# Causal masks from 64 rows in the attention scores of a fused attention and expert kernel

## The chip, the cores and the metric

The kernel runs on one core of a Trainium2 chip. A core has a matrix engine (PE, with its weight loads shown apart as PEld), a vector engine (DVE), a scalar engine (ACT), a general engine (POOL), and a queue engine (SP) that starts the transfers here. Each engine works through its own instructions in order, and engines wait for each other by semaphores. The metric is the time of one execution on the device in microseconds (us); the number compared is a median over runs.

## The reference

What must be computed, cut to what matters:

```python
# 4 batches, 12 heads, 448 positions, 64 dimensions for each head
scores = scale * np.matmul(q, k.transpose(0, 1, 3, 2))
mask = np.triu(np.ones((seq, seq), dtype=bool), k=1)
scores = np.where(mask, -1000000000.0, scores)
scores = scores - np.max(scores, axis=-1, keepdims=True)
attn = np.exp(scores)
attn = attn / (np.sum(attn, axis=-1, keepdims=True) + 1e-09)
x = np.matmul(attn, v)            # then (1792 tokens, 768)
h = np.maximum(np.maximum(x @ w1, x @ w2), x @ w3)
out = h @ w_out
```

Row m of the scores may only see columns up to m. All inputs are float32.

## The kernel before

The 48 heads are worked in 24 pairs; the two heads of a pair lie side by side on the partitions, head 0 on rows 0 to 63 and head 1 on rows 64 to 127. The 448 positions make four blocks of rows: 0, 1 and 2 with 128, and 3 with 64. For each pair the scores come in two groups, each into a PSUM tile S of two banks, one bank for each head:

- Group A (z = 0, function `mm` in `attend`, line 710): blocks 2 (384 columns at 0) and 0 (128 columns at 384).
- Group B (z = 1): block 1 (256 columns at 0) of each head, and block 3 of both heads at once: the 64 last rows of head 0 and of head 1 stand as 128 output rows, with 256 keys in one bank and 192 in the other.

The causal mask is a matrix product that goes into the same PSUM area ahead of the scores: a bf16 identity `identb` (128 × 128) as weights times a constant mask `mk` that holds 0 or −2^104 as the moving operand; the scores then accumulate on top. In group A this is one product of 256 columns for each head (two copies of the 128 × 128 mask, for the diagonals of blocks 2 and 0). In group B it is one of 128 columns for each head, and one for block 3. The scores themselves are fp32; those of blocks 0, 1 and 2 have 64 rows of weights, one head on the upper half of PE's rows and the other on the lower half; those of block 3 have 128 rows.

```python
for h in range(2):
    m(512 * h + 256, 256, identb, mk[:, 0:256], True)      # group A, line 719
...
m(896, 128, identb, mk[:, 256:384])                        # group B, line 723
```

Behind the scores DVE takes the maxima (line 741), ACT the exponentials with their sums (line 752); the first 6 pairs are then transposed on PE (line 766), the later ones are split into two 16-bit halves and transposed by a DMA (line 808). The products with the values fill a tile O (line 828, 16-bit, or 841 for the first pairs): weights of 128 rows and 64 columns, the two heads on different columns of PE. Between them PE works through the hidden products of the experts (line 1030) and the output products (line 1441), and after the last pair through two schemes of combined products for the other batches (lines 1262 and 1387); all these have weights of 128 rows and 128 columns.

What runs when is written down: `ORDER` is a list of all operations and `ENGINE` says which engine takes each. A planner (class `Order`) goes through that list with a cost for each operation and works out a start time, the buffer that each result gets, and the order by start time in which the program is emitted. The cost of the two groups of scores stands ahead of line 733.

The masks are prepared at the start (lines 1507 to 1519) by POOL, while PE runs 13 products of no use on the tile `junk` (line 1501).

Of the kernel before, what the change touches and what calls it, by code (L numbers as in the profile page):

```python
# [9 lines left out]
BF16 = mybir.dt.bfloat16  # L10
I32 = mybir.dt.int32
AF = mybir.ActivationFunctionType
ALU = mybir.AluOpType
AX = mybir.AxisListType

P = 128
D = 64
# [157 lines left out]
    qr=3, kr=3, acc=2, p32=2, ph=2, pT=3, v16=5, vr=4, w3=4, x=4, wst=2, h=6, hacc=4, osb=2, S=2, O=1, M=3,  # L175
# [16 lines left out]
class Order:  # L192
# [31 lines left out]
    def add(self, cost, emit, reads=(), writes=(), ring=None, prio=0.0, lat=None, chain=None, bank=None, port=False):  # L224
        i = len(self.ops)
        deps, behind = set(), set()
        for n in reads:
            deps.update(self.writers.get(n, ()))
        for n in writes:
            deps.update(self.writers.get(n, ()))  # L230
            deps.update(self.readers.get(n, ()))
        for z in (chain, ring[0] if ring and ring[0] in self.FIFO else None):
            if z is not None:
                if z in self.last:
                    behind.add(self.last[z])
                self.last[z] = i
        for n in reads:
            self.readers.setdefault(n, []).append(i)
        for n in writes:
            self.writers[n] = [i]  # L240
            self.readers[n] = []
        if ring is not None:
            self.ring_of[ring[1]] = ring[0]
            if len(ring) == 2:
                self.pending[ring[0]] = self.pending.get(ring[0], 0) + 1
        names = set()
        for n in list(reads) + list(writes) + ([ring[1]] if ring else []):
            names.add(n)
            if isinstance(n, tuple) and isinstance(n[0], tuple):
                names.add(n[0])  # L250
        names = {n for n in names if n in self.ring_of}
        for n in names:
            self.uses[n] = self.uses.get(n, 0) + 1
        self.ops.append(dict(cost=cost, emit=emit, deps=deps, behind=behind - deps, ring=ring, prio=prio, lat=lat, names=names, bank=bank, port=port, group=self.group))
# [146 lines left out]
def c_pe(*cols):  # L401
    return sum(n / 2400 + 0.003 for n in cols)


def c_pe32(*cols):
    return sum(4 * n / 2400 + 0.006 for n in cols)


def c_dma(*parts):

    issue = [0.45 for _ in parts]
    data = sum(n * z for n, z in parts) / 340e3
    return [(e, 0.06 * len(parts), sum(issue), data, False, sum(issue[:-1])) for e in ("sp", "act")]
# [7 lines left out]
def attention_moe(ctx: ExitStack, tc: tile.TileContext, q, k, v, w1, w2, w3, wo, out):  # L421
    nc = tc.nc
    PE, ACT, DVE, POOL, SP = nc.tensor, nc.scalar, nc.vector, nc.gpsimd, nc.sync
# [3 lines left out]
    c1 = ctx.enter_context(tc.tile_pool(name="c1", bufs=1))  # L427
    psp = ctx.enter_context(tc.tile_pool(name="psp", bufs=1, space=PSUM))
    shapes = dict(
        qr=([P, 512], F32), kr=([P, S_LEN], F32), acc=([P, 28], F32), p32=([P, 1024], F32), ph=([P, 16, P], F16),  # L430
# [57 lines left out]
    identb = c1.tile([P, P], BF16, name="identb")  # L488


    mk = c1.tile([P, 3 * P], BF16, name="mk")
    junk = c1.tile([P, 384], F16, name="junk")
    osc = c1.tile([P, 8], F32, name="osc")
    tiny = osc[:, 4:6]
# [14 lines left out]
    add = od.add  # L509
# [4 lines left out]
    def ap(t, off, dims, p0=0, np_=P):  # L514
        s = t.ap[0][0]
        return bass.AP(t.tensor, t.offset + p0 * s + off, [[s, np_]] + [list(d) for d in dims])
# [179 lines left out]
    def attend(b, p, prio, plain):  # L696
        qr, kr, acc, O = ((n, b, p) for n in ("qr", "kr", "acc", "O"))
# [3 lines left out]
        for z, blocks in enumerate(HALVES):  # L701
            od.group = f"{'ab'[z]}{6 * b + p}"
            S, y = ("S", b, p, z), ("p32", b, p, z)
            pr = prio + 0.1 * z
# [5 lines left out]
            def mm(e, z=z, S=S):  # L710
                o, qq, kk = T(S), T(qr), T(kr)

                def m(c, w, l, r, start=False):
                    PE.matmul(o[:, c : c + w], l, r, start=start, stop=True, skip_group_check=True)  # L714


                if z == 0:
                    for h in range(2):
                        m(512 * h + 256, 256, identb, mk[:, 0:256], True)
                else:  # L720
                    for h in range(2):
                        m(512 * h + 128, 128, identb, mk[:, 0:P], True)
                    m(896, 128, identb, mk[:, 256:384])
                    m(256, 256, qq[:, 384:512], kk[:, 0:256])
                    m(768, 192, qq[:, 384:512], kk[:, 256:448])
                for i, c in ((2, 0), (0, 384)) if z == 0 else ((1, 0),):
                    w = P * (i + 1)
                    for h in range(2):
                        hs = slice(D * h, D * h + D)
                        m(512 * h + c, w, qq[hs, P * i : P * i + P], kk[hs, 0:w])  # L730

            cost = c_pe(256, 256) + c_pe32(384, 128) if z == 0 else c_pe(128, 128, 128) + c_pe32(256, 192, 256)
            add([("pe", cost + (0.3 if z == 0 else 0.36))], mm, reads=[qr, kr], writes=[S], ring=("S", S), prio=pr)

            groups = [blocks[0:2], blocks[2:4]] if z == 0 else [blocks[0:2], blocks[2:3]]
            for gi, g in enumerate(groups):

                def mx(e, g=g, S=S):
# [6 lines left out]
                    ring=("acc", acc) if z == 0 and gi == 0 else None, prio=pr, chain=acc, bank=S)  # L745
# [3 lines left out]
            for n, at, parts, c, w in blocks:  # L749

                def ex(e, at=at, parts=parts, c=c, w=w, S=S, y=y):
# [6 lines left out]
                    writes=[(y, n, "e"), (acc, "s", n)], ring=("p32", y) if first else None, prio=pr, chain=y, bank=S)  # L758

            if plain:  # L760
                for g in range(2):
# [6 lines left out]
                    def place(e, g=g, M=M, t=t):  # L768
# [4 lines left out]
                    c = dict(act=c_act(512, -0.09), dve=c_dve(512))  # L773
                    add([(e, c[e]) for e in ENGINES["pT"]], place, reads=[M], writes=[(t, 0, g), (t, 1, g)],
                        ring=("pT", t) if g == 0 else None, prio=pr + 0.4, bank=M, chain=t)
                continue

            def eps(e, cols=cols):
# [4 lines left out]
                writes=[(acc, "r", z)], prio=pr)  # L783
# [12 lines left out]
            def p_lo(e, z=z, y=y):  # L796
# [4 lines left out]
                prio=pr, port=True)  # L801
# [5 lines left out]
            def tr(e, z=z):  # L807
# [3 lines left out]
                ring=("pT", pT[z]), prio=prio + 0.4)  # L811
# [38 lines left out]
        if plain:  # L850
# [18 lines left out]
            def quotient(e):  # L869
# [4 lines left out]
            c = dict(act=c_act(S_LEN, 0.02), dve=c_dve(S_LEN) + 0.06)  # L874
            add([(e, c[e]) for e in ENGINES["R"]], lambda e: scaled(e, T(x32), T(R)[:, 0:S_LEN], bsc[:, b, 10:11]),
                reads=[R, ("scale", b)], writes=[x32], ring=("hacc", x32), prio=prio + 0.6)
            add([("pe", 4 * c_pe(*(6 * [P] + 4 * [D])) + 0.1)], pv_plain, reads=pb + vb, writes=[O], ring=("O", O),
                prio=prio + 0.9)
            add([("dve", c_dve(S_LEN))], quotient, reads=[O], writes=[x32], prio=prio + 0.9)
            add([("act", c_act(S_LEN, -0.045))], lambda e: scaled(e, T(x)[:, kx, 0], T(x32), 1.0), reads=[x32],  # L880
                writes=[(x, kx, 0)], ring=("x", x) if kx == 0 else None, prio=prio + 0.9, chain=x)
            add(c_rest("x lo", S_LEN), lambda e: rest(e, T(x)[:, kx, 1], T(x32), T(x)[:, kx, 0]), reads=[x32, (x, kx, 0)],
                writes=[(x, kx)], prio=prio + 0.9, port=True)
            return

        for z in range(2):
            add([("pe", 3 * c_pe(*(4 * [P] if z == 0 else 2 * [P] + 4 * [D])) + (0.02 if z == 0 else 0.12))], lambda e, z=z: pv(e, z),
                reads=[n for n in pb if n[0] == pT[z]] + vb + [(O, 0)] * z, writes=[(O, z)], ring=("O", O) if z == 0 else None,
                prio=prio + 0.9)
# [614 lines left out]
    DVE.memset(bsc, 0.0)  # L1504
    DVE.memset(tiny[:, 0:1], 1e-9 / PS)
    DVE.memset(tiny[:, 1:2], 1e-9)
    POOL.memset(mk, 0.0)
    for t in (ident, identb):
        POOL.memset(t, 1.0)
    for z in range(2):  # L1510
        POOL.affine_select(
            out=mk[:, P * z : P * z + P], in_=mk[:, P * z : P * z + P], pattern=[[-1, P]], base=0, channel_multiplier=1,
            compare_op=ALU.is_ge, fill=-(2.0**104))
    for t in (identb, ident):
        POOL.affine_select(
            out=t, in_=t, pattern=[[-1, P]], base=0, channel_multiplier=1, compare_op=ALU.is_equal, fill=0.0)
    for h in range(2):
        POOL.tensor_copy(mk[D * h : D * h + D, 256 : 256 + D], mk[0:D, 0:D])
    POOL.memset(mk[:, 256 + D : 384], -(2.0**104))


    u = 0
# [56 lines left out]
```

## Time and profile before

| | |
|---|---|
| median of 3 runs | 464.23 us (463.53 to 465.03) |
| the profiled execution's own time | 464.76 us |
| its span, first to last instruction | 463.1 us |
| mean granted clock of PE | 0.995 |
| PE busy | 453.9 us (98%) |
| DVE busy | 415.0 us (90%) |
| ACT busy | 323.2 us (70%) |
| POOL busy | 149.2 us (32%) |

The span is what the profile covers; the execution's own time has 1.7 us around it. Busy times of PE count each product from its start to the end of its way through the array, so products that follow each other overlap, and the distance from one start to the next tells more than one duration. An fp32 product appears as two instructions. In the chain of waits the profile goes back from the last instruction, at each step to what released it.

### The profile page before, as it was taken

The page shows a single profiled execution, that of the slowest core. Times are in us where ns is not written, and L with a number is a line of the kernel's source. Part 1 is how long each engine was busy: PE and PEld are TensorE (multiplying, and loading weights), DVE is VectorE, ACT ScalarE, POOL GpSimd, SP SyncE. Part 2 cuts the span into 40 slices and gives each one's busy share as a digit, 9 for nine tenths or more (in the row PEclk, how much of TensorE's full clock was granted, in tenths as well). Part 3 has the DMA queues.
Part 4 walks back from the last instruction along what each step waited for, and adds up shares of the span by engine and source line. Part 5 has one row for each costly group of instructions (what it writes and reads, how often), then busy time and mean ns, then how long its engine had stood idle before and what let it go on. Part 6 is the DMA issues. An engine that isn't in the chain of part 4 may idle for free.

```text
span 463.1 us, 9807 instructions
## 1 busy us (share of the span) xinstructions
PE 453.9 (98%) x3705; PEld 266.1 (57%) x3705; DVE 415.0 (90%) x801; ACT 323.2 (70%) x760; POOL 149.2 (32%) x177
## 2 busy tenths in 40 slices
PE   7999999999999999999999999999999999999996
PEld 4778665565665655555665556655555555555553
DVE  3899999999999999996787789889999999999984
ACT  5899999999999989994788577894432334441520
POOL 3115513363545324512234535021032322222030
PEclk9899999999999999999999999999999999999999
DMA  8858367988898899629477654762100000000023
GB/s 228 296 176 269 100 225 226 219 216 180 184 232 236 184 228 239 110 54 185 126 158 163 139 112 88 140 149 67 41 0 2 0 1 1 1 0 2 0 100 139
DMA packets 102319, 60.40 MB, mean 130 GB/s; under 512 B 76672, under 2 KB 99712, under 8 KB 102272
## 3 DMA queue, kind: packets, MB, share of 16 engines
q1 hardware_dynamic: 102272, 59.78, 52.2%
q8 instruction: 29, 0.48, 0.4%
q14 instruction: 18, 0.15, 0.1%
HBM read 35.39 MB, written 5.51 MB: 88 GB/s over the span
## 4 chain that ended last, share of the span: by engine, by line
PE 84%; ACT 9%; DMA 2%; DVE 2%; issue 1%; DVEq 0%; ACTq 0%
PE M L1030 25%; PE L L1262 14%; PE S L714 11%; PE M L1441 9%; PE M L1262 7%; PE O L828 6%; PE L L1387 4%; ACT region L752 4%; PE O L1262 3%; ACT region L520 3%; DMA region<-in_moe_w_dram 2%; PE M L1387 2%; ACT region L953 1%; PE O L1387 1%; PE M L559 1%
## 5 line engine op out<-in xcount | busy, mean ns | idle before, releaser
L1030 PE MATMUL M<-x,w 128*128 128x448 f16 x648 | 128.2, 353 | 0.4 <-POOL x L531 0.4
L1030 PEld LDWEIGHTS <-w 128*128 128x128 f16 x648 | 61.3, 98 | 57.8 <-issue 2.3
L752 ACT ACTIVATE region<-S,acc 128x128 f32<-128x128 f32 (+3 forms) x168 | 82.4, 504 | 10.9 <-DVE acc L741 8.2
L741 DVE TENSOR_REDUCE acc<-S 128x2 f32<-128x512 f32 (+2 forms) x96 | 61.3, 682 | 14.0 <-PE S L714 11.8
L531 POOL TENSOR_TENSOR region<-region 128x1024 f16<-128x1024 f32 x22 | 46.9, 2134 | 73.7 <-ACT region L520 41.3
L714 PE MATMUL S<-region 64*128 64x384 f32 (+4 forms) x384 | 66.8, 406 | 0.0
L520 ACT ACTIVATE region<-region 128x1024 f16<-128x1024 f32 (+3 forms) x58 | 44.6, 777 | 18.5 <-DVE region L1195 6.9
L520 ACT ACTIVATE region<-region,acc 128x384 f32<-128x384 f32 (+3 forms) x93 | 44.3, 530 | 12.1 <-DVE acc L782 12.1
L714 PEld LDWEIGHTS S<-region 64*128 64x128 f32 (+1 forms) x384 | 40.7, 190 | 18.4 <-issue 11.2
L520 ACT ACTIVATE region<-region,cols 128x384 f16<-128x384 f32 (+1 forms) x38 | 22.9, 615 | 37.7 <-DVE region L1120 25.7
L1262 PEld LDWEIGHTS <-region 128*128 128x128 f16 x324 | 31.7, 98 | 29.6
L1115 POOL TENSOR_TENSOR region<-w 128x384 f32<-128x384 f16 x25 | 22.3, 913 | 79.3 <-DVE region L540 26.8
L1441 PE MATMUL M<-h,w 128*128 128x448 f16 x216 | 42.8, 353 | 0.0
L1262 PE MATMUL L<-region,region 128*128 128x448 f16 x207 | 41.3, 353 | 0.0
L1262 PEld LDWEIGHTS <-w 128*128 128x128 f16 x243 | 23.5, 98 | 21.8
L752 ACT ACTIVATION_READ_ACCUMULATOR region<-S,acc 128x1 f32 x168 | 34.7, 207 | 0.0
L1262 PE MATMUL M<-x,w 128*128 128x448 f16 x162 | 32.8, 353 | 0.0
L1441 PEld LDWEIGHTS <-w 128*128 128x128 f16 x216 | 20.4, 98 | 19.5 <-issue 1.0
L828 PEld LDWEIGHTS <-region 128*64 128x64 f16 x1080 | 26.6, 111 | 8.5 <-issue 7.9
L828 PE MATMUL O<-region,region 128*64 128x128 f16 (+1 forms) x1080 | 30.0, 211 | 0.0
L938 DVE TENSOR_SCALAR_CACHE_REDUCE region<-region 128x768 f32<-128x768 f32 x24 | 22.3, 940 | 1.1 <-ACT region L953 1.0
L950 DVE SCALAR_TENSOR_TENSOR region<-region 128x768 int32<-128x768 int32 x24 | 22.8, 955 | 0.3
(175 smaller groups left out, 782.8 us busy)
## 6 DMA issues: line engine op xcount, KB each, us to landing
region<-in_moe_w_dram SPq DMA_DIRECT2D x18, 768.0 KB, 4.8
region<-in_q_dram SPq DMA_DIRECT2D x24, 224.0 KB, 3.3
region<-in_k_dram SPq DMA_DIRECT2D x24, 224.0 KB, 3.9
region<-in_v_dram SPq DMA_DIRECT2D x12, 384.0 KB, 5.8
region<-in_moe_w_out_dram SPq DMA_DIRECT2D x6, 768.0 KB, 4.9
out_dram<-osb SPq DMA_DIRECT2D x15, 224.0 KB, 2.3
out_dram<-region SPq DMA_DIRECT2D x6, 224.0 KB, 2.0
region<-in_v_dram SPq DMA_DIRECT2D x4, 192.0 KB, 4.9
```

Source lines behind the costliest of these rows:

```text
L520: ACT.activation(o, i, AF.Copy, scale=f)
L531: ENG[eng].tensor_tensor(out=o, in0=i, in1=hi, op=ALU.subtract)
L714: PE.matmul(o[:, c : c + w], l, r, start=start, stop=True, skip_group_check=True)
L741: DVE.tensor_reduce(out=T(acc)[:, at : at + len(g)], in_=i, op=ALU.max, axis=AX.XY if parts == 2 else AX.X, negate=True)
L752: ACT.activation(part(T(y), parts, c, w), part(T(S), parts, c, w), AF.Exp, bias=T(acc)[:, at : at + 1], accum_out=T(acc)[:, 7 + at : 8 + at])
L828: PE.matmul(T(O)[D * h : D * h + D, P * i : P * i + w], vt[j][:, vl, (2 * p + h) * D : (2 * p + h + 1) * D], T(pT[u])[:, 8 * pl + c, a : a ...
L938: DVE.tensor_scalar(out=T(x32), in0=T(x32), scalar1=MIN_HI, scalar2=None, op0=ALU.max, op1=ALU.max, accum_out=wmx[:, c])
L950: DVE.scalar_tensor_tensor(out=xi(), in0=word(1), scalar=TOP2, in1=xi(), op0=ALU.bitwise_and, op1=ALU.bitwise_or)
L1030: PE.matmul(T(M)[:, 0:S_LEN], w16[j][:, kk, wl, fs], xx[:, kk % 3, xl], start=(kk == 0 and wl + xl == 0), stop=(kk == 5 and wl == 1))
L1262: PE.matmul(T(M)[:, 0:S_LEN], stat(c, wl), mov(c, xl), start=first and n == 0, stop=n == 8, skip_group_check=True)
L1387: PE.matmul(T(M)[:, 0:S_LEN], stat[0](c, wl), mov[0](c, xl), start=first and c + wl + xl == 0, stop=c == 2 and wl == 1, skip_group_check=True)
L1441: PE.matmul(T(M)[:, 0:S_LEN], w16[3][:, f, wl, es], T(("h", b, f))[:, hl], start=(f == 0 and hl + wl == 0), stop=(f == 5 and wl == 1))
```

## The change

The mask is now made of 64 rows for each head. `mr` (64 × 64 for each head) holds −2^104 where the column is at or behind the row, and 0 elsewhere. `mw` (64 × 192 for each head) has a diagonal that is shifted by 63, and ones in row 0 for the first 64 columns; a cut of 128 columns of it moves the rows of `mr` to where they belong: the cut from 64 serves the first 64 columns of a diagonal block, the cut from 0 the last 64. So a diagonal block is masked in two halves of 64 columns, and each half is one product for each head: head 0 on PE's rows 0 to 63, head 1 on rows 64 to 127, one behind the other in the program. Group A needs four such products of 2 × 64 columns, group B four of 64 columns.

In group B the 64-row work (masks and scores of block 1) now stands first, and the work with 128 rows (the mask and the scores of block 3) behind it. `mk` keeps only the mask of block 3. The planner's costs become two numbers. The preparation is shared by DVE and POOL.

```diff
+A_COST, B_COST = 1.25, 1.69
...
-    mk = c1.tile([P, 3 * P], BF16, name="mk")
+    mk = c1.tile([P, P], BF16, name="mk")
+    mr = c1.tile([P, D], BF16, name="mr")
+    mw = c1.tile([P, 3 * D], BF16, name="mw")
...
-                if z == 0:
+                for half in range(2):
                     for h in range(2):
-                        m(512 * h + 256, 256, identb, mk[:, 0:256], True)
-                else:
-                    for h in range(2):
-                        m(512 * h + 128, 128, identb, mk[:, 0:P], True)
-                    m(896, 128, identb, mk[:, 256:384])
-                    m(256, 256, qq[:, 384:512], kk[:, 0:256])
-                    m(768, 192, qq[:, 384:512], kk[:, 256:448])
+                        hs = slice(D * h, D * h + D)
+                        l, r = mw[hs, D - D * half : D - D * half + P], mr[hs, :]
+                        c = 512 * h + D * half
+                        if z == 0:
+                            PE.matmul(
+                                ap(o, c + 256, [[P, 2], [1, D]]), l, ap(mr, 0, [[0, 2], [1, D]], D * h, D), start=half == 0,
+                                stop=True, skip_group_check=True)
+                        else:
+                            m(c + P, D, l, r, half == 0)
                 for i, c in ((2, 0), (0, 384)) if z == 0 else ((1, 0),):
                     w = P * (i + 1)
                     for h in range(2):
                         hs = slice(D * h, D * h + D)
                         m(512 * h + c, w, qq[hs, P * i : P * i + P], kk[hs, 0:w])
-
-            cost = c_pe(256, 256) + c_pe32(384, 128) if z == 0 else c_pe(128, 128, 128) + c_pe32(256, 192, 256)
-            add([("pe", cost + (0.3 if z == 0 else 0.36))], mm, reads=[qr, kr], writes=[S], ring=("S", S), prio=pr)
+                if z == 1:
+                    m(896, 128, identb, mk)
+                    m(256, 256, qq[:, 384:512], kk[:, 0:256])
+                    m(768, 192, qq[:, 384:512], kk[:, 256:448])
+
+            cost = A_COST if z == 0 else B_COST
+            add([("pe", cost)], mm, reads=[qr, kr], writes=[S], ring=("S", S), prio=pr)
...
-    POOL.memset(mk, 0.0)
+    DVE.memset(mr, 0.0)
+    DVE.memset(mw, 0.0)
...
-    for z in range(2):
+    NEG = -(2.0**104)
+    for h in range(2):
+        hs = slice(D * h, D * h + D)
         POOL.affine_select(
-            out=mk[:, P * z : P * z + P], in_=mk[:, P * z : P * z + P], pattern=[[-1, P]], base=0, channel_multiplier=1,
-            compare_op=ALU.is_ge, fill=-(2.0**104))
+            out=mr[hs, :], in_=mr[hs, :], pattern=[[-1, D]], base=-1, channel_multiplier=1, compare_op=ALU.is_ge, fill=NEG)
+        POOL.affine_select(
+            out=mw[hs, :], in_=mw[hs, :], pattern=[[-1, 3 * D]], base=D - 1, channel_multiplier=1, compare_op=ALU.not_equal,
+            fill=1.0)
+        DVE.memset(mw[D * h : D * h + 1, 0:D], 1.0)
...
+    DVE.memset(mk, NEG)
     for h in range(2):
-        POOL.tensor_copy(mk[D * h : D * h + D, 256 : 256 + D], mk[0:D, 0:D])
-    POOL.memset(mk[:, 256 + D : 384], -(2.0**104))
+        hs = slice(D * h, D * h + D)
+        DVE.memset(mk[hs, 0:D], 0.0)
+        POOL.affine_select(
+            out=mk[hs, 0:D], in_=mk[hs, 0:D], pattern=[[-1, D]], base=0, channel_multiplier=1, compare_op=ALU.is_ge, fill=NEG)
```

On PE, in group A of pair 8 (the ninth; it stands between hidden products of line 1030), the order before was this; S is the tile of scores, `region` holds q and k, `w` the experts' weights:

```order
L1030 LDWEIGHTS w_2_95
L1030 MATMUL M_90<-x_68,w_2_95 128x448
L714 LDWEIGHTS identb
L714 MATMUL S_91<-mk,identb 128x256
L714 LDWEIGHTS identb
L714 MATMUL S_91<-mk,identb 128x256
L714 MATMUL S_91<-region_65 128x384 x2
L714 MATMUL S_91<-region_65 128x128 x2
L1030 LDWEIGHTS w_0_93
```

In the same place of PE's order there now stands:

```order
L1041 MATMUL M_90<-x_68,w_2_95 128x448
L728 LDWEIGHTS mw
L728 MATMUL S_91<-mr,mw 128x2x64
L728 LDWEIGHTS mw
L728 MATMUL S_91<-mr,mw 128x2x64
L728 LDWEIGHTS mw
L728 MATMUL S_91<-mr,mw 128x2x64
L728 LDWEIGHTS mw
L728 MATMUL S_91<-mr,mw 128x2x64
L719 MATMUL S_91<-region_65 128x384 x2
L719 MATMUL S_91<-region_65 128x128 x2
L1041 LDWEIGHTS w_0_93
```

Two masks of 256 columns over 128 rows became four of 128 columns over 64 rows, the first and third for head 0, the others for head 1; the scores behind them are the same.

On PE, in group B of the same pair (also between hidden products), the order before was:

```order
L714 LDWEIGHTS identb
L714 MATMUL S_92<-mk,identb 128x128
L714 LDWEIGHTS identb
L714 MATMUL S_92<-mk,identb 128x128
L714 LDWEIGHTS identb
L714 MATMUL S_92<-mk,identb 128x128
L714 MATMUL S_92<-region_65 128x256
L714 MATMUL S_92<-region_65 128x192
L714 MATMUL S_92<-region_65 128x256 x2
L1030 LDWEIGHTS w_1_94
L1030 MATMUL M_90<-x_68,w_1_94 128x448
```

Now, from the second of the four small masks on:

```order
L719 LDWEIGHTS mw
L719 MATMUL S_92<-mr,mw 128x64
L719 LDWEIGHTS mw
L719 MATMUL S_92<-mr,mw 128x64
L719 LDWEIGHTS mw
L719 MATMUL S_92<-mr,mw 128x64
L719 MATMUL S_92<-region_65 128x256 x2
L719 LDWEIGHTS identb
L719 MATMUL S_92<-mk,identb 128x128
L719 MATMUL S_92<-region_65 128x256
L719 MATMUL S_92<-region_65 128x192
L1041 LDWEIGHTS w_1_94
```

The two 64-row scores (`128x256 x2`) moved from the end of the group to behind the small masks, and the products over 128 rows now end it. Elsewhere PE's order is unchanged.

## Rows read from the trace of the kernel before

**Rows 1.** The profile's page, part 1: busy us, share of the span, instructions

```profile
PE 453.9 (98%) x3705; PEld 266.1 (57%) x3705; DVE 415.0 (90%) x801; ACT 323.2 (70%) x760; POOL 149.2 (32%) x177
```

**Rows 2.** Busy time by stretch (us, PE, weight loads, DVE, ACT, POOL, clock, DMA)

```profile
0.00:78.00 78.00, 73.03 (x683) 51.94 (x683) 67.44 (x140) 70.24 (x186) 26.20 (x52) 0.98 0.72 223
78.00:200.00 122.00, 121.58 (x1068) 71.71 (x1069) 117.39 (x235) 116.77 (x258) 53.73 (x49) 1.00 0.85 194
200.00:464.00 264.00, 259.28 (x1957) 142.47 (x1955) 230.22 (x427) 136.21 (x318) 69.30 (x76) 1.00 0.32 73
```

**Rows 3.** The chain that ended last: start us, us, what

```profile
58.54 0.92 ACT region L953
...
78.43 0.93 PE M L559 x6
...
84.80 1.28 PE S L714 x10
...
297.77 3.00 PE S L714 x21
```

**Rows 4.** Timeline of PE around 85 us: start us, us, engine, line, operation

```profile
84.64 0.38 PE L714 MATMUL S<-mk,identb 128*128 128x256 bf16 x2
84.95 1.14 PE L714 MATMUL S<-region 64*128 64x384 f32 x8
86.02 0.36 PE L1030 MATMUL M<-x,w 128*128 128x448 f16 x1
```

**Rows 5.** Timeline of PE's weight loads in the same place

```profile
84.95 0.95 PEld L714 LDWEIGHTS S<-region 64*128 64x128 f32 x8 [0.21 <-issue]
```

**Rows 6.** Timeline of PE, the second pass of the same products

```profile
85.38 0.49 PE L714 MATMUL S<-region 64*128 64x384 f32 x2
```

**Rows 7.** Timeline of PE around 93 us

```profile
92.96 0.33 PE L714 MATMUL S<-mk,identb 128*128 128x128 bf16 x3
93.12 1.61 PE L714 MATMUL S<-region 128*128 128x256 f32 x8
94.67 0.36 PE L1030 MATMUL M<-x,w 128*128 128x448 f16 x1
```

**Rows 8.** Timeline of PE around 100 us

```profile
98.75 0.38 PE L714 MATMUL S<-mk,identb 128*128 128x256 bf16 x2
...
100.13 0.34 PE L714 MATMUL S<-mk,identb 128*128 128x128 bf16 x3
100.31 1.61 PE L714 MATMUL S<-region 128*128 128x256 f32 x8
101.84 0.25 PE L828 MATMUL O<-region,region 128*64 128x128 f16 x2
```

**Rows 9.** Timeline of PE around 199 us

```profile
199.09 0.39 PE L828 MATMUL O<-region,region 128*64 128x128 f16 x8
199.41 0.39 PE L714 MATMUL S<-mk,identb 128*128 128x256 bf16 x2
```

**Rows 10.** PE's weight loads by shape: busy us, mean ns

```profile
L714 PEld LDWEIGHTS S<-region 64*128 64x128 f32 x288 | 24.3, 189 | 17.1 <-issue 11.2
...
L714 PEld LDWEIGHTS S<-region 128*128 128x128 f32 x96 | 16.4, 191 | 1.2
...
L714 PEld LDWEIGHTS <-identb 128*128 128x128 bf16 x120 | 9.5, 98 | 5.7 <-issue 0.5
```

**Rows 11.** Timeline of DVE and of PE before 131.5 us

```profile
129.63 1.01 DVE L540 SCALAR_TENSOR_TENSOR w<-region,wf,w 128x768 f16<-128x768 f32 x1
...
131.12 0.54 PE L1030 MATMUL M<-x,w 128*128 128x448 f16 x2
```

**Rows 12.** Timeline of POOL in the first 4 us

```profile
1.54 0.54 POOL L1511 TENSOR_SCALAR_AFFINE_SELECT mk<-mk 128x128 bf16<-128x128 bf16 x2
...
2.52 0.52 POOL L1518 COPY mk<-mk 64x64 bf16<-64x64 bf16 x2
...
3.52 0.23 POOL L690 COPY region<-region 64x64 f32<-64x64 f32 x1 [0.28 <-DMA region<-in_q_dram]
```

## The prediction

> **What bounds the kernel now.** I read the busy shares first, then the stretches, the chain, and single instructions of PE. Over the whole span PE is busy 98% and DVE 90% [rows 1]. From 78 us to the end PE is busy without a pause, and before 78 us it has pauses, while ACT and DVE are nearly full until 200 us [rows 2]. "Busy" is weak evidence for a pipelined engine, so the chain decides: up to 78 us it hops between ACT, DVE and weight DMAs; from 78.43 us on the pieces are PE, one behind the other, until the last result is evicted [rows 3]. So PE time saved after 78 us counts in full as long as the other engines still hand over in time, and PE time saved before counts little.
>
> The scores (S, line 714) stand in that chain in 25 pieces, the first at 84.80 and the last at 297.77 us [rows 3]. They hold 32 of the 48 score groups: an A group is the first half of a pair of heads (blocks 2 and 0), a B group the second (blocks 1 and 3).
>
> **What one group costs now.** An A group takes 86.02 − 84.64 = 1.38 us [rows 4]. Two masks stream 256 columns each, 2 × 0.107 = 0.21 us at the granted clock of 1.00 (2.4 GHz) [rows 2, 4], which ends at 84.85. The first score starts at 84.95, so PE stood still for 0.10 us: its loads of 64-row weights came only after the 128-row masks had run out (idle 0.21 before them) [rows 5]. I call this a drain. The second pass of the scores starts 0.43 us after the first [rows 4, 6], though two heads side by side, two passes of 384 columns, need 0.32: 0.11 us of fp32 weight load lies open. Four passes of 512 columns are 0.85 us, and what is left, 0.10, is the drain back to 128 rows. A B group takes 94.67 − 92.96 = 1.71 us with two drains as well: three masks of 128 columns at 0.055 [rows 7], the 128-row scores, a drain, the 64-row scores, a drain. A drain also follows the products of the values (O, 128 rows by 64 columns): eight of them start at 199.09, in four pairs of 0.053 they end at 199.30, and the mask comes at 199.41 [rows 9].
>
> After a drain a 16-bit load costs nearly nothing: three masks take 0.18 us behind one (100.13 to 100.31) [rows 8] and 0.16 to 0.17 without (92.96 to 93.12) [rows 7], so 0.01.
>
> **The change, part by part.** No row shows a 16-bit load of 64 rows. The nearest are three: fp32 with 64 rows 189 ns, fp32 with 128 rows 191 ns, bf16 with 128 rows 98 ns [rows 10]. Rows do not matter there and the type does, so I price the new loads like the 128-row bf16 ones (0.01 open after a drain, renewed every 0.055 us); the other end is the fp32 one, 0.11 open each time. That two row halves run side by side I take from the fp32 scores: 0.85 us are four passes of 512 columns once, not for each head.
>
> The Trainium skill says the same in "TensorE: Matmul & The Clock Gate", section on weight-path perf modes: a fast weight load is used when 128 weights of a type other than FP32 are loaded, and a load's time goes by columns. For 128 rows the trace agrees (98 against 191 ns); for 64 rows no run here shows it. By that rule the sum is the one below, without it the rival "slow loads".
>
> A group, neighbours of 128 × 128:
> - masks: 512 columns in a row become 256, two halves side by side: −0.107.
> - the fp32 load can be fetched while the second pair of masks (0.053) runs, as nothing changes shape between them: 0.11 open becomes 0.055: −0.055.
> - the drain moves ahead of the masks, and the number of drains stays; the first 16-bit load lies open: +0.01.
>
> Together −0.15. After O products the old order drained twice ahead of the scores (O to 128 rows, 128 to 64), the new one once, and the 0.01 was there already: −0.26.
>
> B group, same neighbours: three masks of 0.16 us become one of 0.053 and two pairs of 64 columns. A pair is bounded by its columns (0.027) and by the load's pace (0.055); I take 0.04, so 0.13: −0.03. The open fp32 load falls from 0.11 to 0.07: −0.04. Two 16-bit loads now come after a drain: +0.02. Together −0.05. B now ends in 128-row work where it ended in 64-row work. So by neighbours: O before it, −0.16 (a drain less); O behind it, +0.05 (a drain more). Right behind an A group, the drain between them goes: A and B together −0.42 with 128-row work next, −0.32 with O next.
>
> Counting the 25 pieces of the chain by what stands before and behind them: 7 A with −0.15 (1.05), 2 A after O (0.52), 6 A+B before O (1.92), one A+B before 128-row work (0.42), 4 B (0.20), 4 B after O (0.64), one B before O (−0.05). Sum 4.70 us of PE time after 78 us.
>
> What the others give back: at 131.12 PE uses a weight plane that DVE finished at 130.64 [rows 11], 0.48 us ahead, and DVE is busy 117.4 of 122 us between 78 and 200 [rows 2]. By 150 us the sum has reached 1.47. If DVE cannot move at all, 0.48 of that survives and the total is 0.48 + 3.23 = 3.7; if it moves along fully, 4.7. DVE waits partly for PE itself, so I take 4.0. From 200 us DVE is busy 230 of 264 us [rows 2] and follows PE.
>
> Before 78 us 16 groups stand. With the plain terms they save at most 8 × 0.15 + 8 × 0.05 = 1.6 us of PE time, at least 0; as the chain lies on ACT and DMA, I take 0.2.
>
> The preparation: POOL loses a memset, two selects of 128 × 128 (0.27 each), two copies and a memset, and gets six selects on 64 rows; DVE gets seven small memsets. At most 6 × 0.27 = 1.6 us of selects stand against 0.54 + 0.52 and two memsets, and behind them waits only the copy in q, which idled 0.28 us for its DMA [rows 12]. PE runs its warm-up products until 4.8 us, so I cost it at 0; without that cover up to 0.3 us of the start. No DMA is added or moved. The new costs shift only the times that the planner reckons with: the order on SP and ACT stays as it is, and on DVE and POOL behind the preparation. The new order inside B lets nobody start earlier: its maxima wait for the whole group as before.
>
> Total −4.2 us. The profiled execution took 464.76 us (span 463.1), so 460.6; it lay 0.53 above the median of 464.23, so against the median I predict 460.0.
>
> **Rivals.**
> - One after another: the 16-bit masks of the two halves do not overlap. Then A gives back 0.107 and B 0.08: 16 × 0.187 = 3.0 us, gain 1.2 to 1.7, 462.7 us. For it: nothing in the trace shows bf16 on half the rows. Against: fp32 does overlap in the same shape.
> - The others hold PE up until 200 us: only 0.48 us survives from there, and 2.56 us of the sum lies behind it: gain 3.0, 461.2 us. For it: ACT and DVE at 96% [rows 2]. Against: they hand over early enough everywhere that PE never idles. The Trainium skill warns of this in "TensorEngine Tiling (Array Packing)", "PSUM Bottleneck": faster TensorE can leave evacuation as the limit. The trace does not show it as a wait after 78 us.
> - Slow loads, side by side: 0.107 open for both pairs and the scores, 0.32 per group where I have about 0.17: 32 × 0.15 = 4.8 us, which eats the gain. No change, 464.2 us.
> - Slower: slow loads one after another. Four times 0.107 and the fp32 load make 0.53 per group instead of 0.17, 32 × 0.36 = 11.5 us against 4.7: 471 us. It decides from 0.13 us more per group than I have. Against: the scores' own 64-row loads run in pairs, or 0.43 us between their passes would be more.
>
> **How the numbers follow.** Forecast 0.68 (its own range 458.9 to 461.0: a gain of 5.3 is 4.7 and a third of the early 1.6; one of 3.2 is the 3.7 from above, less 16 × 0.015 where B's pairs take 0.055, less 32 × 0.01 where the open load is 0.02), others hold up 0.11, one after another 0.10, slow loads 0.06, slower 0.05. A difference under 0.3% (1.4 us) cannot be told from none here. Faster than that: 0.68 + 0.11 + 0.06 of the masks one after another = 0.85; within 0.10; slower 0.05. The range reaches to 462.8, which takes in the masks one after another, and down to 458.8.
>
> **What would show it.** Right: A groups between 128-row work take about 1.23 us from the end of the work ahead, A+B before O 2.78 where it was 3.09 (101.84 − 98.75) [rows 8]; the 64-row bf16 loads last near 98 ns; the chain is PE from about 78 us. Wrong: loads near 190 ns, or the second head's mask starting 0.05 us after the first's, or new idle time of PE before weight planes of line 1030 between 120 and 200 us.

## The result, and the profile after

The changed kernel took 459.88 us in the median of four runs (459.21 to 461.64), the kernel before 464.63 (463.53 to 467.11). The ratio is 0.989, with an interval of 0.9857 to 0.9924. The prediction was 460.0, from 458.8 to 462.8. A second set gave 460.0 against 465.37, ratio 0.9886 (0.9853 to 0.9920).

The profiled execution took 459.21 us, its span is 457.5. First the busy shares, as in [rows 1], and the three stretches of [rows 2] with the same columns:

```profile
PE 447.5 (98%) x3801; PEld 261.3 (57%) x3801; DVE 415.7 (91%) x808; ACT 322.9 (71%) x760; POOL 148.7 (32%) x177
```

```profile
0.00:78.00 78.00, 72.36 (x734) 51.20 (x735) 69.22 (x149) 71.77 (x189) 26.31 (x52) 1.00 0.71 224
78.00:200.00 122.00, 121.44 (x1139) 71.19 (x1135) 117.49 (x235) 117.27 (x258) 52.88 (x49) 1.00 0.84 194
200.00:464.00 264.00, 253.73 (x1937) 138.86 (x1935) 229.02 (x426) 133.86 (x315) 69.48 (x76) 0.99 0.33 73
```

PE has 96 products more and 6.4 us less busy time, and its share is still 98%. The shares alone would say that nothing changed in kind. The chain says otherwise (start us, us, what; its longest pieces):

```profile
91.10 1.83 ACT region L763 x8
...
127.88 0.93 DVE w L545
...
135.83 0.94 DVE w L545
...
143.55 1.03 DVE w L545
144.62 6.61 PE M L1041 x34
151.45 0.92 PE S L719 x8
```

Before, the pieces were PE from 78.43 us on [rows 3]. Now ACT and DVE hold the end until 144.62, and PE takes over only there. Lines have moved by 5 or by 11: 719 was 714 and 545 was 540, 1041 was 1030 and 763 was 752; 728 is the new mask of an A group.

PE around an A group, which answers to [rows 4, 6], and its weight loads, which answer to [rows 5] (timelines: start, us, engine, line, operation):

```profile
82.42 0.73 PE L1041 MATMUL M<-x,w 128*128 128x448 f16 x3
83.08 0.28 PE L728 MATMUL S<-mr,mw 64*128 64x128 bf16 x4
83.20 1.09 PE L719 MATMUL S<-region 64*128 64x384 f32 x8
84.22 0.55 PE L1041 MATMUL M<-x,w 128*128 128x448 f16 x2
```

```profile
83.08 0.11 PEld L728 LDWEIGHTS <-mw 64*128 64x128 bf16 x4 [0.37 <-issue]
83.15 0.95 PEld L719 LDWEIGHTS S<-region 64*128 64x128 f32 x8
```

From the first mask to the next work 1.14 us, where 1.38 stood. The pause of 0.10 between masks and scores is gone; it now stands ahead of the masks: the last product ahead starts at 82.79 and streams its 448 columns until 82.98 (at 2.4 GHz), the mask starts at 83.08. The score's load is fetched while the second pair of masks runs, with no idle time before it.

A B group between 128-row work, which answers to [rows 7], and A and B together with O next, which answer to [rows 8]:

```profile
91.25 0.23 PE L719 MATMUL S<-mr,mw 64*128 64x64 bf16 x4
91.32 0.68 PE L719 MATMUL S<-region 64*128 64x256 f32 x4
91.93 0.23 PE L719 MATMUL S<-mk,identb 128*128 128x128 bf16 x1
92.00 0.98 PE L719 MATMUL S<-region 128*128 128x256 f32 x4
92.81 0.73 PE L1041 MATMUL M<-x,w 128*128 128x448 f16 x3
```

```profile
96.98 0.28 PE L728 MATMUL S<-mr,mw 64*128 64x128 bf16 x4
97.10 1.08 PE L719 MATMUL S<-region 64*128 64x384 f32 x8
98.02 0.22 PE L719 MATMUL S<-mr,mw 64*128 64x64 bf16 x4
98.08 0.68 PE L719 MATMUL S<-region 64*128 64x256 f32 x4
98.69 0.23 PE L719 MATMUL S<-mk,identb 128*128 128x128 bf16 x1
98.75 0.98 PE L719 MATMUL S<-region 128*128 128x256 f32 x4
99.66 1.57 PE L839 MATMUL O<-region,region 128*64 128x128 f16 x60
```

B takes 92.81 − 91.25 = 1.56 us and 0.09 of pause ahead of it; A and B 99.66 − 96.98 = 2.68 and the same pause, 2.78 in all, where it was 3.09. Between A and B there is no pause.

The weight loads by shape, as in [rows 10] (busy us, mean ns):

```profile
L719 PEld LDWEIGHTS S<-region 64*128 64x128 f32 x288 | 23.9, 189 | 6.4 <-issue 0.2
L719 PEld LDWEIGHTS S<-region 128*128 128x128 f32 x96 | 16.6, 193 | 1.2
L719 PEld LDWEIGHTS <-mw 64*128 64x128 bf16 x96 | 3.5, 94 | 4.1 <-issue 3.7
L728 PEld LDWEIGHTS <-mw 64*128 64x128 bf16 x96 | 2.7, 95 | 6.9 <-issue 6.5
```

The new loads of 64 rows in bf16 last 94 and 95 ns.

Last the hand-over of [rows 11]: DVE's plane and the product behind it, and the one other place between 78 and 160 us where PE waits:

```profile
127.80 1.01 DVE L545 SCALAR_TENSOR_TENSOR w<-region,wf,w 128x768 f16<-128x768 f32 x1
128.73 0.15 DVE L981 TENSOR_REDUCE cols<-wt 128x1 f32<-128x3 f32 x1
```

```profile
127.93 0.55 PE L1041 MATMUL M<-x,w 128*128 128x448 f16 x2
128.86 6.61 PE L1041 MATMUL M<-x,w 128*128 128x448 f16 x34 [0.38 <-DVE cols L981]
144.62 6.61 PE L1041 MATMUL M<-x,w 128*128 128x448 f16 x34 [0.18 <-DVE w L545]
```

PE had 0.48 us in hand there and now waits. The product starts at 128.86, 0.05 behind the end of the plane (128.81); the reduction that the page names signals only at 128.88, so it was the plane that released PE. The page counts idle time from the end of the product ahead, 0.36 us behind that one's start, while without a wait the next product starts 0.19 behind it. By starts the two places cost more than the 0.38 and 0.18 of the page: 0.55 and 0.34 us against before, 0.89 in all.

**Where the 5.6 us between the two spans are.** I measured when the first score of each A group starts, against the same score of before. The ninth starts at 84.95 us in before [rows 4] and 1.75 us sooner after; the end comes 5.55 us sooner. So 3.80 lie behind that score. The ninth group has by then saved 0.09 of its own (from the end of the work ahead to the score 0.31 us before and 0.22 now), so with all of that group it is 3.89. In a second profile of the changed kernel the ninth group was 0.19 us sooner and the end 4.00, again 3.81. What repeats is 3.8; the first 85 us differ by 1.6 us between two profiles of one kernel.

### The profile page after: what moved, and what is told of

It reads as the page before. It is cut to its first block, busy times and chain, and to the rows that moved or that the text cites. A ratio compares the mean times of both kernels' runs of the same rounds, so it can differ in the third digit from the quotient of the medians.

```text
span 457.5 us, 9999 instructions
## 1 busy us (share of the span) xinstructions
PE 447.5 (98%) x3801; PEld 261.3 (57%) x3801; DVE 415.7 (91%) x808; ACT 322.9 (71%) x760; POOL 148.7 (32%) x177
## 4 chain that ended last, share of the span: by engine, by line
PE 75%; ACT 12%; DVE 8%; issue 2%; DMA 1%; POOL 1%; SPq 0%; ACTq 0%
PE M L1041 16%; PE L L1273 14%; PE M L1452 9%; PE S L719 8%; PE M L1273 7%; ACT region L525 5%; PE L L1398 4%; PE O L839 4%; ACT region L763 4%; PE O L1273 3%; PE M L1398 2%; PE M L777 2%; PE O L852 2%; DVE region L949 1%; ACT region L964 1%
## 5 line engine op out<-in xcount | busy, mean ns | idle before, releaser
L719 PE MATMUL S<-region 64*128 64x384 f32 (+4 forms) x384 | 65.1, 392 | 0.0
L763 ACT ACTIVATION_READ_ACCUMULATOR region<-S,acc 128x1 f32 x168 | 36.7, 220 | 0.0
```

Of the source, the lines that this page charges most:

```text
L763: ACT.activation(part(T(y), parts, c, w), part(T(S), parts, c, w), AF.Exp, bias=T(acc)[:, at : at + 1], accum_out=T(acc)[:, 7 + at : 8 + at])
```

## The experiments

Theory: the sum of 4.70 us is right, side by side and with cheap loads, and DVE takes some 0.7 of it back before 150 us. Rivals: the two halves run one after another; the others hold PE until 200 us; the gain comes from somewhere else, the start above all. The kernels of the table are described below it. Shifts are us against before of the first score of the ninth, twelfth, fourteenth and sixteenth A group (at 84.95, 127.11, 153.58, 199.74 in before), and of the end:

| kernel | 85 | 127 | 154 | 200 | end |
|---|---|---|---|---|---|
| changed | −1.75 | −2.57 | −2.30 | −2.90 | −5.55 |
| changed, again | −0.19 | −0.90 | −0.73 | −1.35 | −4.00 |
| late_pairs | +0.24 | +0.24 | −0.17 | −0.79 | −3.44 |
| early_pairs | −1.45 | −2.25 | −0.78 | −0.79 | −0.78 |
| heads_apart | −1.30 | −2.08 | −1.72 | −1.91 | −4.50 |
| one_head | −0.46 | −1.21 | −0.99 | −1.62 | −4.20 |
| wide_first | −2.45 | −2.87 | −2.88 | −3.41 | −5.31 |
| relief_before | +0.32 | +0.32 | +0.32 | +0.32 | +0.33 |
| relief_after | −2.51 | −3.35 | −3.83 | −4.46 | −7.10 |

**Half of the pairs each.** The new masks and order from pair 12 on only, or in pairs 0 to 11 only. In the other pairs the old instructions run, on a mask tile whose pattern is not the causal one; sizes and types are the old ones.

```diff
-                for half in range(2):
+                u = 6 * b + p
+                new = u >= 12 if z == 0 else u >= 12
+                if new:
+                    for half in range(2):
...
+                elif z == 0:
                     for h in range(2):
+                        m(512 * h + 256, 256, identb, ap(mk, 0, [[0, 2], [1, P]]), True)
```

That is late_pairs; early_pairs has `u < 12` in place of `u >= 12`.

> New masks and new order only from pair 12 on (from 142 us of the kernel before); pairs 0 to 11 keep 128-row masks in the old order (their mask has the right size and a wrong pattern). Theory 'PE counts after the hand-over': all the PE time saved there survives, 3.5 us faster than before (ratio 0.9925), about four fifths of the whole change. Rival 'the early pairs count too' (the profile after is already 1.56 us ahead at 85 us): at most 2.7 us faster.

> New masks and order only in pairs 0 to 11; the later ones keep 128-row masks in the old order (right size, wrong pattern). Theory: PE saves about 2.7 us up to 130 us, but ACT and DVE set the pace until 145 us, so 0.5 to 0.8 us of it is left at the end (ratio 0.9985). Rival 'the early pairs count too': 1.6 to 2.7 us faster. If PE's clock makes the early difference, the stretch up to 20 us is 1.2 us shorter or longer from profile to profile with the clock, whatever the masks.

Measured: late 461.18 us against 465.22 (ratio 0.9918, 0.9885 to 0.9951), early 463.53 (0.9967, 0.9944 to 0.9990). The late pairs keep all that they save: 3.68 us from the twelfth A group on. The early ones are 2.25 us ahead at 127 us, lose 1.47 of it by 154 us, and keep 0.78. PE's timeline of the early kernel shows the loss (line 1053 is the changed kernel's 1041):

```profile
129.19 6.61 PE L1053 MATMUL M<-x,w 128*128 128x448 f16 x34 [0.39 <-DVE cols L993]
136.71 0.49 PE L564 MATMUL M<-ident,wmx 128*128 128x128 f32 x2 [0.47 <-DVE region L961]
146.04 6.60 PE L1053 MATMUL M<-x,w 128*128 128x448 f16 x34 [0.22 <-DVE w L545]
```

Three waits for DVE stand between 129 and 146 us, 1.08 us on the page. By starts against before, the three places lose 0.55, 0.73 and 0.39 us, and the lead falls from 2.48 us, behind the last new group, to 0.79: the waits are the whole loss. So time that PE saves before 127 us is mostly worth nothing, and what it saves later counts. The medians alone wouldn't show it: early's lies 1.7 us below before's, which would fit the rival, and in runs of one granted clock (the start, below) it is 1.0. But in the profile the lead shrinks from 1.45 us at 85 us to 0.78 at the end: behind 85 us the new groups bring nothing that lasts.

**One kind of group each.** The new form in A groups only, or in B groups only, made in the same way.

```diff
+                new = True if z == 0 else False
```

```diff
+                new = False if z == 0 else True
```

> New masks in the A groups alone; the B groups keep the old order and 128-row masks (right size, wrong pattern for block 1). Theory of drains and side-by-side masks: A takes 1.23 us from the end of the 128-row work ahead (1.38 before), also ahead of B, no drain between A and B goes; 2.6 us of PE time after 78 us, 2.3 us at the end (ratio 0.995). Rival 'the order of B does it all': under 1 us.

> New masks and new order in the B groups alone; the A groups keep 128-row masks (right size, wrong pattern). Theory: B alone between 128-row work 1.66 us from the end of the work ahead (1.71 before), the drain between A and B goes; 2.1 us of PE time after 78 us, 1.8 us at the end (ratio 0.996). Both parts together should add up to the whole. Rival 'masks of A do it all': under 0.5 us.

Measured: A 461.34 us (0.9919, 0.9890 to 0.9948), B 462.31 (0.9953, 0.9930 to 0.9976). Both help, A more, as the terms say. But the medians lie 3.9 and 2.9 us below before's 465.22, which adds up to 6.8 where both together give 5.4. Compared in runs of one granted clock (the start, below) it is 3.2 and 2.25 against 4.5, so 1.0 too much. The profiles show where this excess isn't. Counted from the work ahead of the ninth A group, A alone gains 2.28 us to the end (2.3 expected), B alone 1.60 (1.8 expected), 3.88 together; both at once gain 3.89. So behind 85 us the parts add up, and each comes out near its forecast. The rest lies in the first 85 us, where A alone is 1.55 us ahead of before, B alone 1.18, and the two profiles of the changed kernel 1.66 and 0.09; why the start varies so stays open.

**The changed kernel again, and the order of its products.** The first as it is; the second with the two halves of a head behind each other in the program instead of the two heads.

```diff
-                for half in range(2):
-                    for h in range(2):
+                for h in range(2):
+                    for half in range(2):
```

> The changed kernel itself once more, beside the kernel before on the same chip, to have the whole gain to well under a third of a per cent and more profiles of the start. Theory: 4.2 us (ratio 0.991), with a spread of 1 to 1.5 us from where PE's clock falls in the first 20 us.

> The changed kernel with the four small masks in another order: both halves of head 0, then both of head 1. Theory 'side by side': the two products on the same rows must follow each other (0.055 us in A, about 0.03 in B), only the middle two overlap, so A groups are about 0.05 us longer and B groups about 0.03. Rival 'only the number of columns counts': no difference, 1.14 and 1.56 us from the first mask to the next work.

Measured: 460.0 us, as in the first set; heads apart 460.25 in a single run. I expected the new order to cost something and it cost nothing: A 1.140 to 1.143 us from the first mask, B 1.561, A and B 2.687, against 1.139, 1.558 and 2.684. In this order the first two products lie on the same 64 rows. Single starts in the trace are 140.867, 140.874, 140.934 and 140.940 us: two at once, then two at once. Products on the same rows follow each other by 0.06 us here, so the two that start 7 ns apart lie on different halves. From that I infer that the third of the program started ahead of the second: each half of the rows works off its own products. That run lost 0.4 us more between 154 and 200 us than the others. Its groups are no longer; three hidden products, at 159.64, 179.60 and 190.01 us, start 0.07, 0.14 and 0.22 us late against before. What they wait for was not followed.

**The 128-row products of a B group first, as in before, with the new masks.**

```diff
+                if z == 1:
+                    m(896, 128, identb, mk, True)
+                    m(256, 256, qq[:, 384:512], kk[:, 0:256], True)
+                    m(768, 192, qq[:, 384:512], kk[:, 256:448])
                 for half in range(2):
...
```

> The changed kernel with the 128-row part of each B group (mask and scores of block 3) placed first again, small masks and 64-row scores behind. Theory of drains: B alone between 128-row work the same to 0.05 us; behind an A group one drain more (A+B before O 0.10 us longer than the 2.68 of the changed kernel, before 128-row work 0.2 longer); B after O 0.10 longer; B before O 0.10 shorter. Sum of PE time after 78 us about 1.1 us more than in the changed kernel. Rival 'the masks alone do it': no difference in A+B.

Measured: 459.44 us in a single run. PE's timeline, where A and B stand together with O next:

```profile
96.49 0.28 PE L732 MATMUL S<-mr,mw 64*128 64x128 bf16 x4
96.61 1.08 PE L719 MATMUL S<-region 64*128 64x384 f32 x8
97.63 0.23 PE L719 MATMUL S<-mk,identb 128*128 128x128 bf16 x1
97.69 0.98 PE L719 MATMUL S<-region 128*128 128x256 f32 x4
98.60 0.23 PE L719 MATMUL S<-mr,mw 64*128 64x64 bf16 x4
98.67 0.68 PE L719 MATMUL S<-region 64*128 64x256 f32 x4
99.28 1.57 PE L839 MATMUL O<-region,region 128*64 128x128 f16 x60
```

99.28 − 96.49 = 2.79 us instead of 2.68: a pause between A and B again. With 128-row work next it is 0.20 longer, since the end of B needs one too. A B group alone between 128-row work stays the same to 0.01; behind O it is 0.10 longer, and ahead of O 0.11 shorter. All this is as expected. So the new order of B is worth one or two pauses of 0.10 beside an A group, one behind O, nothing between 128-row work, and costs one ahead of O. From the ninth A group to the end this run gains 2.86 us where the changed kernel gains 3.80; its low time comes from the start (−2.45 at 85 us). As a single run it says nothing against the new order.

**The mask of one head only.** Head 1 keeps no mask in blocks 0, 1 and 2: that part of the computation is left out.

```diff
                 for half in range(2):
-                    for h in range(2):
+                    for h in range(1):
...
-                        m(512 * h + c, w, qq[hs, P * i : P * i + P], kk[hs, 0:w])
+                        m(512 * h + c, w, qq[hs, P * i : P * i + P], kk[hs, 0:w], h == 1 and i > 0)
```

> The changed kernel with the small masks of head 0 alone; head 1's blocks 0, 1 and 2 go unmasked (their scores start the bank). Half of the small masks' columns and loads are gone. Theory 'side by side': head 1's masks ran in the shadow of head 0's, so an A group keeps its 1.14 us and a B group between 128-row work its 1.56 us, to 0.01. Rival 'one after another': A falls by 0.107 to 1.03, B by 0.05 to 0.08.

Measured: A 1.133 to 1.136 us, B 1.554, A and B 2.680; 460.57 us in a single run. Halving the mask products changes a group by 0.003 to 0.006 us, where in series it would be 0.1. The second head's masks cost nothing beside the first's. The first products of an A group:

```profile
84.48 0.23 PE L728 MATMUL S<-mr,mw 64*128 64x128 bf16 x1
84.49 0.59 PE L719 MATMUL S<-region 64*128 64x384 f32 x1
84.54 0.22 PE L728 MATMUL S<-mr,mw 64*128 64x128 bf16 x1
84.60 1.08 PE L719 MATMUL S<-region 64*128 64x384 f32 x7
```

Here the two masks, both of head 0, stand in the program ahead of all scores. But one score starts at 84.49, between them: it can only be head 1's, which has no mask to wait for. That shows directly what the starts of heads_apart let me infer.

**DVE relieved, in both kernels.** The pass of the dequantisation that puts in the last three bits works on 96 columns instead of 768; the rest of the weights keep those bits at zero.

```diff
-                out=xi(), in0=word(0), scalar=29, in1=xi(), op0=ALU.logical_shift_right, op1=ALU.bitwise_or)
+                out=xi()[:, 0:96], in0=word(0)[:, 0:96], scalar=29, in1=xi()[:, 0:96], op0=ALU.logical_shift_right, op1=ALU.bitwise_or)
```

> The kernel before with one DVE pass over the weights (line 946, the last three bits) cut from 768 to 96 columns, so DVE has some 0.8 us less for each of 24 weights, 9 of them between 85 and 154 us; the other columns keep those bits zero. Theory: in that stretch PE sets the pace of the kernel before, so from the ninth A group (84.95) to the fourteenth (153.58) it stays at 68.6 us, to 0.2. Rival 'DVE sets it already': some us shorter.

> The changed kernel with the same cut of that DVE pass. Theory: with DVE relieved, all the PE time saved between the ninth and the fourteenth A group (1.5 us) shows: 67.1 to 67.3 us from the one to the other, where the changed kernel takes 68.1; what DVE gave back in that stretch comes through. Rival 'ACT holds the stretch, not DVE': it stays at 68.0.

Measured: 465.12 us for before with the relief, 457.66 for the changed kernel, one run each. The stretch from the ninth to the fourteenth A group is 68.63 us in before and stays 68.63 with relief; it is 68.08 in the changed kernel and falls to 67.31. The chain of the relieved changed kernel:

```profile
75.35 0.62 ACT hacc L525
76.02 0.93 PE M L564 x6
76.95 0.79 PE O L839 x24
77.75 4.65 PE M L1041 x24
```

The chain is PE from 76.02 us to the end, and the page has no wait of PE between 84 and 200 us. From the ninth group's score to the end it gains 7.10 − 2.51 = 4.59 us on before, and the same relief in before gains nothing (0.01). The changed kernel keeps 3.80 of the 4.59, so DVE takes back 0.79. That is a lower bound, since the relief isn't complete: by starts PE still loses 0.14 at the first plane, which ends at 127.62 with its product at 127.68. PE's own sum can also be added up from the starts of the products behind each of the 25 pieces, against before: 7 A groups at 0.145 to 0.147, 2 A after O at 0.252, 6 A and B before O at 0.316 to 0.318, one before 128-row work at 0.412, 4 B at 0.054 to 0.056, 4 B after O at 0.159 to 0.162, one B before O at −0.041, and 0.103 of which I had no term (below). It comes to 4.77. The changed kernel keeps 3.89 and loses 0.89 in the two waits.

## Why the prediction was right

**A groups.** Predicted 1.23 us from the end of the work ahead; 1.237. By its parts: 0.097 of pause, 0.121 for the masks (0.107 and 0.014 of open load, where I had 0.01), 0.379 between the first two score passes (0.32 and 0.055 predicted). Right in each.

**A and B together.** Predicted 2.78 us from the end of the work ahead with O next, a gain of 0.32; measured 2.778, 0.317. With 128-row work next the gain was to be 0.42, and is 0.412 (2.591 from the first mask and 0.098 of pause ahead of it).

**B alone.** 1.71 less 0.05 is 1.66; 1.656. Its mask pairs start 0.040 and 0.029 us apart, where I took 0.04 for each. That the loads would not set the pace at 0.055 was chosen between bounds, and came out on the good side. One piece gained more than its term: behind the B group at 185 us stand fp32 products over 128 rows, and the second of them comes another 0.103 sooner. I read the 0.10 as their open fp32 load, which now has no pause ahead of it; no run separates it.

**Loads.** 94 and 95 ns against 98. I had the row on bf16 and the row on 64 rows, and no row on both; the type decided, not the rows. The two rivals on slow loads are out. By the rule of the Trainium skill in "TensorE: Matmul & The Clock Gate", section on weight-path perf modes, a load's time goes by columns and the type admits the fast form; the trace now agrees for 64 rows by 128 columns too.

**Side by side.** The rival "one after another" needed A groups 0.107 longer; one_head and the starts 3 ns apart (83.079 and 83.082) rule it out.

**What the others give back.** I priced DVE's hand-over at 131 us at 0.7 of 4.70, so 4.0 kept; measured 0.89 of 4.77, 3.89 kept. The place was right: waits for DVE at 128.86 and 144.62, of which the relieved kernel keeps 0.14. The size was too small: of the 1.46 saved by 150 us 0.56 survives, close to the 0.48 of my bound where DVE cannot move at all, and not the 0.8 that 4.0 implies. The 0.103 above makes up for half of it, by luck. Under what would show me wrong I had named new idle time before those planes; it came, and it was what my own term had priced, so as a sign it was badly chosen. The rival in which the others hold PE until 200 us is out: the chain is PE from 144.62, late_pairs gains 3.68, and from 154 us to the end the changed kernel gains 3.25 us where the relieved one gains 3.27.

**The chain, wrong.** I wrote that PE would be the chain from about 78 us. But where PE waits for DVE at 131 us, the chain runs through DVE there, and back from it through the work of DVE and ACT to before 78 us. The two statements did not fit each other; the term was right and what I said of the chain wrong.

**The start, mis-sized.** I took 0.2 us of at most 1.6. The timed runs bear more. With each run goes its mean granted clock, and in runs at 0.998 or above the means are 464.38 us for before (18 runs) and 459.90 for the changed kernel (9): 4.48, with some 0.3 of uncertainty. Less the 3.89 behind 85 us, 0.6 is left for the start. The changed kernel's medians lie 4.75 and 5.4 below, since more runs of before have a lower clock (below). So −4.2 was made of a main term 0.1 too high and a start some 0.4 too low. The start varies by more than either from run to run, so that the total came within 0.1 us of the median is in part luck.

**Preparation.** Costed at nothing, and the first score came 0.53 us later (5.65 instead of 5.12 us), more than the 0.3 I had as the price without cover. PE's idle time before its products at 9.5 us is 1.00 instead of 1.73, so that was made up by there.

Two versions were not tried. A mixed order of B, wide part first only where O follows and no A stands ahead, would save about 0.1 us in all. Putting a B group right behind an A group is worth more: between 128-row work the two together gain 0.412 where apart they gain 0.145 and 0.055, so some 0.2 for a pair. That is an estimate from these rows, and it would shift the planner's order.

## What to carry to other kernels

Price a change on TensorE by what stands before and behind each group, not by columns alone: here a change between 64-row and 128-row products cost 0.10 us each time, an fp32 load left open 0.11, and the columns saved were only some 0.11 of an A group's 0.15 to 0.26. Then look for the first place where the engine that feeds PE has less in hand than PE will have gained by there; time saved ahead of that place is lost but for what is in hand there (here 0.56 of 1.46 us survived), and time saved behind it counts in full. The relieved pair of kernels is a cheap way to show it: take the same work from the feeding engine before and after the change, and the difference of the two is the give-back, as far as the relief goes. Where a wait has shifted starts, compare the starts of the same product in both profiles; the idle times of the page were too small here.

## What was not expected of the hardware

**Halves of the rows work off their own products.** one_head shows a 64-row product of one half (84.49) starting ahead of one of the other half (84.54) that stands before it in the program, and the starts of heads_apart fit the same. So it holds for each half of the rows by itself, and not for PE as a whole, that its products start in the order of the program. The order between the halves cost a group at most 0.004 us.

**The clock near the start differs from run to run.** The first 20 us by stretch, of before and then of the changed kernel; the mean granted clock is the third number from the end, with the columns of [rows 2]:

```profile
0.00:20.00 20.00, 16.73 (x129) 11.19 (x129) 11.57 (x29) 13.08 (x38) 5.94 (x24) 0.91 0.93 288
```

```profile
0.00:20.00 20.00, 17.45 (x153) 11.48 (x153) 13.55 (x38) 14.65 (x43) 6.05 (x24) 1.00 0.90 296
```

In before's profile the granted clock is full from 4.27 us, half (1.2 GHz) from 11.10 to 14.51, after PE had idled 1.73 us ahead of 9.70 and 0.36 more ahead of 10.61, and then full. The A group at 11.32 took 2.57 us there, and 1.14 us in the changed kernel, at 11.14. In the timed runs of before the mean of those at 0.997 or below is 466.17 us (16 runs), 1.8 more than of the others; of the changed kernel's ten runs one is such a run. Every other kernel here but relief_before has the new preparation. Of the 36 timed runs with the old one and a clock on record 17 are at 0.997 or below, of the 50 with the new one 11; the profile of relief_before has a stretch at half clock too (11.55 to 14.97), the ten profiles with the new preparation have none there. So such runs came less often with the new preparation here. Whether PE's shorter idle time is why no run here tells. Whoever compares medians should count such runs on both sides: here they make 4.5 us look like 4.75 to 5.4.
